# Layer two's down product in 512 columns: high and low weight parts side by side in one moving operand

## The chip, the cores and the metric

The kernel runs on one core of one Trainium2 chip. The metric is the device time of one execution in microseconds. TensorE (PE) multiplies; each product is a weight load (PEld) of the stationary operand and a MATMUL in which the moving operand streams past. VectorE (DVE) and ScalarE (ACT) do the elementwise work, GpSimd (POOL) issues the indirect DMAs, SyncE (SP) the direct ones.

## The reference, cut to what matters

Three blocks in a row over 24576 tokens (8 x 3072) of 256 features, all in float32:

```python
X = rfft(x, axis=1); y = irfft(X * (filt_r + 1j * filt_i))   # filter along the sequence
e = argmax(y @ w_gate); h = relu(y @ w1[e]); z = gate * eom * (h @ w2[e])   # layer one: 8 experts, 256 -> 1024 -> 256
h = maximum(z @ w_in, 0); out = (h * h) @ w_out   # layer two: 256 -> 2048 -> 256
```

Layer two is the one that the change touches: `w_in` is 256 x 2048 and `w_out` 2048 x 256, and both arrive as float64.

## The kernel before

Filter and routing come first, then layer one sorted by expert, then layer two over the tokens in sorted order. Layer one ends at about 1800 us of the profiled span; the rest is layer two, 48 tiles (`NTILE2`) of 512 tokens.

Every large product is made of three: an operand is split into a high part in the type that TensorE multiplies (`fp32r`) and a low part, the rest, and the kernel computes high x high + low x high + high x low. So `w_out` is held as `woh` and `wol`, and the squared activations `q` as `hh` and `hl` (line 912 on ScalarE, line 914 on VectorE).

A tile's 2048 hidden features are done in 8 units of 256 (`NU`). `steps_m` runs over the 384 units and in each step interleaves three of them, in four parts: `up2` of unit n, `split_h` of unit n-1, `down2` of unit n-2. The schedule is manual: each engine executes in the order in which the code issues, and each waits on semaphores for the data of the others.

- `up2` is a Strassen-like scheme: 7 products of 128 x 128 by 256 columns, 21 matmuls at line 881, stationary from `wsh`/`wsl`, moving from `bh`/`bl`. They go into three PSUM banks: V (`ph`), G (`px`), P (`ph`). Between them ScalarE copies (lines 888, 890, 895, 903) and VectorE adds (line 893 in part 1; lines 899 and 900 in part 2) form the four column blocks `C`. The last product of V (part 3) goes into the bank that line 899 reads, so it comes behind line 899. Line 905 (`q`, part 3) squares.
- `split_h` issues line 912 (ScalarE) in part 1 and line 914 (VectorE) in part 2, behind what `up2` issued there.
- `down2` does 24 matmuls of 256 columns at line 927. The stationary operand is a block of 128 x 128 of `hh` or `hl` (two blocks of hidden features, four blocks of tokens), the moving one a row block of `woh` or `wol`, 256 columns. The four token blocks accumulate over the tile's 8 units in two PSUM banks of 512 columns, two blocks in each; `py_tiles` alternates between two pairs of banks from tile to tile. In the last unit of a tile ScalarE copies each full bank to `ou` (line 933, 512 columns; the first is issued in part 2, the second in part 3), and GpSimd writes it out by four indirect DMAs (line 936).

The parts of `down2` end behind m = 2, 8 and 17, so parts 0 to 3 hold 3, 6, 9 and 6 of its matmuls, beside 6, 6, 6 and 3 of `up2`.

Where the operands lie: the pools on the right side of SBUF are stacked, and `open_m2` puts `pad2` (16 floats, 64 bytes) ahead of the pools of layer two. In the addresses that result, `bh`, `bl`, `hh` and `hl` of layer two begin 64 bytes past a multiple of 128, while `wsh`, `wsl`, `woh`, `wol` begin on multiples of 128. So in `up2` the moving operand is the one that is shifted, in `down2` the stationary one. In layer one (lines 802 and 819) both operands of every matmul begin on multiples of 128; there the moving operand has 512 columns in the wide tiles and 256 in the narrow ones.

Of the kernel before, what the change touches and what calls it, by code (L numbers as in the profile page):

```python
# [12 lines left out]
F32 = mybir.dt.float32  # L13
F32R = mybir.dt.float32r
# [3 lines left out]
ALU = mybir.AluOpType  # L18
# [4 lines left out]
B, S, D = 8, 3072, 256  # L23
NT = B * S
E, F1 = 8, 1024
F2 = 2048
# [4 lines left out]
TT = 512  # L31
# [71 lines left out]
def spectral_moe_kernel(ctx: ExitStack, tc: tile.TileContext, x, filt_r, filt_i, w_gate, w_og, w1, w2,  # L103
                        w_in, w_out, c_ma, c_mi, c_mb, c_mb2, c_sg, c_cum, out):
    nc = tc.nc
# [6 lines left out]
    outv = dram_disjoint_views(out, NT // 128)  # L112
# [49 lines left out]
    pl = {"xsm": ctx.enter_context(tc.tile_pool(name="xsm", bufs=2, side="right"))}  # L162
# [455 lines left out]
    w2nd, lpool = [], []  # L618
    dcs = ctx.enter_context(ExitStack())

    def decode(pool, src, parts, val=None):


        v = nc.vector
        raw = pool.tile([128, ND, 2], I32, name="raw")
        nc.sync.dma_start(out=raw, in_=src)
        yield
        H, L = raw[:, :, 1], raw[:, :, 0]
        ea = pool.tile([128, ND], I32, name="ea")
        eb = pool.tile([128, ND], I32, name="eb")  # L630
        v.tensor_scalar(ea, H, 20, 0x7FF, op0=ALU.logical_shift_right, op1=ALU.bitwise_and)
        v.tensor_scalar(eb, ea, 896, 0, op0=ALU.subtract, op1=ALU.max)
        v.tensor_scalar(ea, eb, 255, None, op0=ALU.min)
        v.tensor_scalar(eb, ea, 23, None, op0=ALU.logical_shift_left)
        yield
        v.tensor_scalar(ea, H, -2147483648, None, op0=ALU.bitwise_and)
        v.tensor_tensor(eb, ea, eb, ALU.bitwise_or)
        yield
        v.tensor_scalar(ea, H, 0xFFFFF, 3, op0=ALU.bitwise_and, op1=ALU.logical_shift_left)
        mb_ = pool.tile([128, ND], I32, name="mb_")  # L640
        v.tensor_scalar(mb_, ea, 0x3F800000, None, op0=ALU.bitwise_or)
        P = eb.bitcast(F32)
        a = pool.tile([128, ND], F32, name="a")
        v.tensor_tensor(a, mb_.bitcast(F32), P, ALU.mult)
        yield
        v.tensor_scalar(ea, L, 1, None, op0=ALU.logical_shift_right)
        lf = pool.tile([128, ND], F32, name="lf")
        v.tensor_scalar(lf, ea, 2.0 ** -51, None, op0=ALU.mult)
        v.tensor_tensor(lf, lf, P, ALU.mult)
        yield  # L650
        if val is not None:
            v.tensor_tensor(val, a, lf, ALU.add)
        for at, hi, lo in parts:
            v.tensor_tensor(hi, a[:, at], lf[:, at], ALU.add)
            v.tensor_tensor(a[:, at], a[:, at], hi.bitcast(F32), ALU.subtract)
            v.tensor_tensor(lo, a[:, at], lf[:, at], ALU.add)
        yield

    def decode_all():
        wres = ctx.enter_context(tc.tile_pool(name="wres", bufs=1))  # L660


        wsh, wsl = (wres.tile([128, F2 // 256, 7, 128], F32R, name=n) for n in ("wsh", "wsl"))
        woh, wol = (wres.tile([128, F2 // 128, D], F32R, name=n) for n in ("woh", "wol"))
        w2nd.extend((wsh, wsl, woh, wol))
        lpool.append(ctx.enter_context(tc.tile_pool(name="rp2", bufs=2)))
        pool = dcs.enter_context(tc.tile_pool(name="dcp", bufs=1))
        first, second = slice(0, 128), slice(128, 256)
        for u in range(F2 // 256):
            a0, a1 = (pool.tile([128, ND], F32, name=f"val{c}") for c in range(2))  # L670
            for c, val in enumerate((a0, a1)):
                yield from decode(pool, w_in32[c * 128:(c + 1) * 128, 2 * u * ND:2 * (u + 1) * ND]
                                  .rearrange("p (n two) -> p n two", two=2),
                                  [(at, wsh[:, u, i], wsl[:, u, i])
                                   for at, i in (((first, 0),), ((first, 1), (second, 2)))[c]], val)
            sc = pool.tile([128, 4, 128], F32, name="sc")
            v.tensor_tensor(sc[:, 0], a0[:, second], a1[:, second], ALU.add)
            v.tensor_tensor(sc[:, 1], sc[:, 0], a0[:, first], ALU.subtract)
            v.tensor_tensor(sc[:, 2], a0[:, first], a0[:, second], ALU.subtract)
            v.tensor_tensor(sc[:, 3], a1[:, first], sc[:, 1], ALU.subtract)  # L680
            yield
            nc.scalar.copy(wsh[:, u, 3:7], sc)
            v.tensor_tensor(wsl[:, u, 3:7], sc, wsh[:, u, 3:7].bitcast(F32), ALU.subtract)
            yield
        for f in range(F2 // 128):
            yield from decode(pool, w_out32[f * 128:(f + 1) * 128].rearrange("p (d two) -> p d two", two=2),
                              [(slice(0, D), woh[:, f, :], wol[:, f, :])])


    psm = ctx.enter_context(ExitStack())  # L690
# [18 lines left out]
    def py_tiles(t):  # L709
        return [pl["psY2" if t % 2 and "psY2" in pl else "psY"].tile([128, TT], F32, name=f"py{h}") for h in range(2)]  # L710
# [6 lines left out]
    slot, k = [], 0  # L717
# [120 lines left out]
    NU = F2 // 256  # L838
    R, X2, H2, Z = {}, {}, {}, {}

    def open_m2():
        right(ctx, "pad2", 1).tile([128, 16], F32, name="pad2")
        for name, bufs in (("bp", 2), ("tp2", 1), ("sp", 2), ("cp", 2), ("h2p", 3), ("oup", 2)):
            pl[name] = right(ctx, name, bufs)

    def load_t(t):
        r = lpool[0].tile([128, 2, TT], F32, name="r")
        nc.sync.dma_start(out=r, in_=ytd[:, t * TT:(t + 1) * TT].rearrange("(h p) t -> p h t", p=128))
        ix = lpool[0].tile([128, 4], I32, name="ix", bufs=4)
        nc.sync.dma_start(out=ix, in_=idsc[t * TT:(t + 1) * TT, 0:1].rearrange("(c p) o -> p (c o)", p=128))  # L850
        R[t] = r, ix
# [66 lines left out]
    def down2(t, u):  # L918

        hh, hl = H2[t, u]  # L920
        woh, wol = w2nd[2:4]
        if u == 0:
            Z[t] = [p.rearrange("p (c d) -> p c d", c=2) for p in py_tiles(t)]
        for m in range(24):
            k, i, c, n = m // 12, m // 6 % 2, m // 3 % 2, m % 3
            x, w = ((hh, woh), (hl, woh), (hh, wol))[n]
            nc.tensor.matmul(Z[t][k][:, c, :], x[:, 2 * i + k, c * 128:(c + 1) * 128], w[:, 2 * u + i, :],  # L927
                             start=u == 0 and m in (0, 12), stop=u == NU - 1 and m in (11, 23), skip_group_check=True)
            if u == NU - 1 and m in (11, 23):
                if k == 0:  # L930
                    Z[t].append(pl["oup"].tile([128, 4, D], F32, name="ou"))
                ou = Z[t][2]
                nc.scalar.copy(ou[:, 2 * k:2 * k + 2, :], Z[t][k])  # L933
                io = X2[t][2]
                for c in range(2 * k, 2 * k + 2):
                    nc.gpsimd.indirect_dma_start(out=outv[4 * t + c], out_offset=bass.IndirectOffsetOnAxis(ap=io[:, c:c + 1], axis=0),  # L936
                                                 in_=ou[:, c, :], in_offset=None)
            if m in (2, 8, 17):
                yield
        del H2[t, u]  # L940
        if u == NU - 1:
            del X2[t], Z[t]
        yield
# [59 lines left out]
    def steps_m():  # L1003
# [15 lines left out]
        m1.close()  # L1019
        xgs.close()  # L1020
        open_m2()
        st = split_t(0)
        for _ in st:
            pass
        for n in range(len(units2) + 2):
            g = up2(*units2[n]) if n < len(units2) else iter(())
            t, u = units2[min(n, len(units2) - 1)]
            d = down2(*units2[n - 2]) if n >= 2 else iter(())
            for part in range(4):
                next(g, None)  # L1030
                if part == 0 and 0 < n <= len(units2):
                    sh = split_h(*units2[n - 1])
                if part in (1, 2) and n:
                    next(sh, None)
                next(d, None)
            if u == 2 and t + 2 < NTILE2:
                load_t(t + 2)
            if u == 3 and t + 1 < NTILE2:
                st = split_t(t + 1)
            next(st, None)  # L1040
            yield
# [43 lines left out]
    m = steps_m()  # L1085
# [4 lines left out]
    for i, k in enumerate(order):  # L1090
# [3 lines left out]
        n = done["a"]  # L1094
# [24 lines left out]
    tables()  # L1119
    open_left()  # L1120
    dec.append(decode_all())
    for _ in m:
        pass
# [33 lines left out]
```

## Time and profile before

| what | value |
|---|---|
| time, median of 3 runs | 3821.22 us (3819.11 to 3822.73) |
| the profiled execution: its own time | 3831.18 us |
| its span | 3829.5 us |
| granted TensorE clock, mean | 0.994 |
| TensorE busy | 3762.7 us, 98% |
| VectorE busy | 2767.0 us, 72% |
| ScalarE busy | 1973.5 us, 52% |
| first matmul of `down2` | 1812.8 us |

The profiled execution is 10 us longer than the median of the runs, and 1.7 us longer than its own span. A busy TensorE says little by itself, since a MATMUL's length in the trace (0.28 us for 256 columns) covers its way through the array, and the next starts long before it ends. What counts for a stream of matmuls is the distance from one start to the next, which the timeline gives.

### The profile page before, as it was taken

What the parts mean: (1) busy time and instruction counts of PE and PEld (TensorE: products, weight loads), DVE (VectorE), ACT (ScalarE), POOL (GpSimd) and SP (SyncE); (2) the same over time, 40 slices, a digit from 0 to 9 for tenths busy, and PEclk for the clock granted to TensorE, in tenths of its full rate; (3) what the DMA queues carried; (4) which work ended last, traced back from release to release, by engine and by line L of the source; (5) the groups of instructions that cost most, each with busy time, mean ns of one, the idle gap of its engine ahead of it and who ended that gap; (6) DMA issues with size and microseconds to landing.
All of it is one profiled execution on the core that took longest, in us unless ns stands there. A gap on an engine that the chain in (4) does not pass through costs nothing.

```text
span 3829.5 us, 73425 instructions
## 1 busy us (share of the span) xinstructions
PE 3762.7 (98%) x27256; PEld 3512.9 (92%) x27256; DVE 2767.0 (72%) x5038; ACT 1973.5 (52%) x3909; POOL 608.2 (16%) x641
## 2 busy tenths in 40 slices
PE   8999999999999999999999999999999999999998
PEld 7888877788888888888999999999999999999998
DVE  6678685688888866655777777777777777777776
ACT  6466463354545545544555555555555555555554
POOL 3477575000000000000001100100110010011001
PEclk9999999999999999999999999999999999999999
DMA  6333322455555545543010010001001000100100
GB/s 194 100 117 113 105 86 91 142 158 165 170 163 173 178 150 161 164 148 114 23 29 23 29 29 23 29 23 29 23 29 29 23 29 23 29 23 29 29 18 18
DMA packets 262750, 309.30 MB, mean 81 GB/s; under 512 B 75153, under 2 KB 206194, under 8 KB 262386
## 3 DMA queue, kind: packets, MB, share of 16 engines
q1 hardware_dynamic: 242928, 252.39, 21.8%
q0 software_dynamic: 18432, 51.93, 3.8%
q8 instruction: 215, 3.52, 0.4%
q14 instruction: 149, 1.22, 0.1%
q10 hardware_dynamic: 1026, 0.23, 0.0%
HBM read 224.01 MB, written 80.45 MB: 80 GB/s over the span
## 4 chain that ended last, share of the span: by engine, by line
PE 37%; issue 14%; POOL 2%; DVE 0%; ACT 0%; POOLq 0%; DVEq 0%; ACTq 0%
PE py L927 20%; PE ph L881 13%; PE px L881 5%; POOL out_dram L936 2%; DVE tc L867 0%; DVE bl L871 0%; DVE hl L914 0%; DVE bl L861 0%; ACT bh L869 0%; POOLq L1152 0%; DVE C L899 0%; ACT ou L933 0%; ACT bh L860 0%; ACT u L895 0%; DVE C L900 0%
## 5 line engine op out<-in xcount | busy, mean ns | idle before, releaser
L927 PE MATMUL py<-woh,hh 128*128 128x256 f32 x3072 | 857.2, 279 | 0.0
L927 PE MATMUL py<-woh,hl 128*128 128x256 f32 x3072 | 852.8, 278 | 0.4 <-DVE hl L914 0.4
L927 PE MATMUL py<-wol,hh 128*128 128x256 f32 x3072 | 852.9, 278 | 0.0
L936 POOL DMA_INDIRECT out_dram<-ou,ix x192 | 214.0, 1115 | 2935.7 <-ACT ou L933 2891.8
L927 PEld LDWEIGHTS py<-woh,hl 128*128 128x128 f32 x3072 | 579.9, 189 | 0.9 <-DVE hl L914 0.8
L927 PEld LDWEIGHTS py<-woh,hh 128*128 128x128 f32 x3072 | 579.9, 189 | 0.0
L927 PEld LDWEIGHTS py<-wol,hh 128*128 128x128 f32 x3072 | 576.3, 188 | 0.0
L806 ACT ACTIVATE hh<-ph 128x512 fp32r<-128x512 f32 (+1 forms) x472 | 251.8, 533 | 586.3 <-PE ph L802 559.3
L881 PE MATMUL ph<-bh,wsh 128*128 128x256 f32 x1920 | 541.5, 282 | 5.6 <-ACT bh L860 4.4
L881 PE MATMUL ph<-bh,wsl 128*128 128x256 f32 x1920 | 539.2, 281 | 0.0
L881 PE MATMUL ph<-bl,wsh 128*128 128x256 f32 x1920 | 539.0, 281 | 0.0
L905 DVE SCALAR_TENSOR_TENSOR q<-C 128x1024 f32<-128x1024 f32 x384 | 468.3, 1220 | 2.3 <-ACT C L903 2.2
L808 DVE SCALAR_TENSOR_TENSOR hl<-ph,hh 128x512 fp32r<-128x512 f32 (+1 forms) x472 | 286.8, 608 | 253.4 <-ACT hh L806 248.5
L914 DVE TENSOR_TENSOR hl<-q,hh 128x1024 fp32r<-128x1024 f32 x384 | 467.1, 1217 | 1.1 <-ACT hh L912 1.1
L899 DVE TENSOR_TENSOR C<-ph,p 128x256 f32<-128x256 f32 x384 | 163.5, 426 | 417.1 <-ACT hh L912 412.8
L903 ACT COPY C<-ph 128x256 f32<-128x256 f32 x384 | 143.0, 372 | 519.7 <-PE ph L881 518.2
L912 ACT CAST hh<-q 128x1024 fp32r<-128x1024 f32 x384 | 403.1, 1050 | 1.3 <-DVE q L905 1.3
L881 PEld LDWEIGHTS ph<-bh,wsh 128*128 128x128 f32 x1920 | 363.0, 189 | 6.9 <-issue 4.6
L881 PEld LDWEIGHTS ph<-bl,wsh 128*128 128x128 f32 x1920 | 361.6, 188 | 0.0
L881 PEld LDWEIGHTS ph<-bh,wsl 128*128 128x128 f32 x1920 | 361.5, 188 | 0.0
L819 PE MATMUL py<-hh,wh 128*128 128x512 f32 (+1 forms) x944 | 348.4, 369 | 0.0
L802 PE MATMUL ph<-xh,wh 128*128 128x512 f32 (+1 forms) x944 | 340.3, 360 | 0.0
(261 smaller groups left out, 8184.2 us busy)
## 6 DMA issues: line engine op xcount, KB each, us to landing
r<-in_moe_w_dram SPq DMA_DIRECT2D x448, 256.0 KB
xt<-in_x_dram SPq DMA_DIRECT2D x48, 512.0 KB
r<-ytd SPq DMA_DIRECT2D x48, 512.0 KB
xg<-srt SPq DMA_DIRECT2D x41, 544.0 KB
ytd<-yt SPq DMA_DIRECT2D x41, 512.0 KB
xg<-srt SPq DMA_DIRECT2D x18, 272.0 KB
ytd<-yt SPq DMA_DIRECT2D x18, 256.0 KB
raw<-in_moe_w_in_dram SPq DMA_DIRECT2D x16, 256.0 KB
```

The lines of the kernel that those rows point to most:

```text
L802: nc.tensor.matmul(ps, a[:, c, f2 * 128:(f2 + 1) * 128], b[:, c, 0:w], start=n == 0, stop=n == 5)
L806: nc.scalar.activation(hh, ps, AF.Relu)
L808: nc.vector.scalar_tensor_tensor(hl, ps, 0.0, hh.bitcast(F32), op0=ALU.max, op1=ALU.subtract)
L819: nc.tensor.matmul(Y[t][h], a[:, f % 2, h * 128:(h + 1) * 128], b, start=f == 0 and i == 0, stop=f == NF - 1 and i == 2)
L881: nc.tensor.matmul(ps, x[:, u, a], y[:, b], start=start and n == 0, stop=n == 2, skip_group_check=True)
L899: nc.vector.tensor_tensor(C[:, 3], V, p5, ALU.add)
L903: nc.scalar.copy(C[:, 2], V)
L905: nc.vector.scalar_tensor_tensor(q, C, 0.0, C, op0=ALU.max, op1=ALU.mult)
L912: nc.scalar.copy(hh, q)
L914: nc.vector.tensor_tensor(hl, q, hh.bitcast(F32), ALU.subtract)
L927: nc.tensor.matmul(Z[t][k][:, c, :], x[:, 2 * i + k, c * 128:(c + 1) * 128], w[:, 2 * u + i, :], start=u == 0 and m in (0, 12), stop=u == ...
L936: nc.gpsimd.indirect_dma_start(out=outv[4 * t + c], out_offset=bass.IndirectOffsetOnAxis(ap=io[:, c:c + 1], axis=0), in_=ou[:, c, :], in_o ...
```

## The change

The two parts of `w_out` become one tile, `wo`, in which a row block's 256 high columns and 256 low columns lie side by side. `hh` now meets both in one matmul of 512 columns, whose result is 256 columns of hh x high and 256 of hh x low in one bank; `hl` meets the high half in a matmul of 256 columns that adds to the first half of the bank. So 16 matmuls replace 24, over the same number of columns (8 x 512 + 8 x 256 = 24 x 256). Each token block has a bank to itself, and every tile uses all four banks (`psY` and `psY2`). The parts now end behind m = 1, 5 and 11. In the last unit of a tile the two halves have to be added: ScalarE copies the first half to `ou` (256 columns), VectorE adds the second half to it, then GpSimd writes the block out; all this four times, the first time behind m = 5, in part 1. `open_m2` gets a second pad of 64 bytes ahead of the pools `h2p` and `oup`, which puts `hh` and `hl` on multiples of 128 bytes; `bh` and `bl` stay where they are.

```diff
--- before.py
+++ after.py
@@ -661,8 +661,8 @@
 
 
         wsh, wsl = (wres.tile([128, F2 // 256, 7, 128], F32R, name=n) for n in ("wsh", "wsl"))
-        woh, wol = (wres.tile([128, F2 // 128, D], F32R, name=n) for n in ("woh", "wol"))
-        w2nd.extend((wsh, wsl, woh, wol))
+        wo = wres.tile([128, F2 // 128, 2, D], F32R, name="wo")
+        w2nd.extend((wsh, wsl, wo))
         lpool.append(ctx.enter_context(tc.tile_pool(name="rp2", bufs=2)))
         pool = dcs.enter_context(tc.tile_pool(name="dcp", bufs=1))
         first, second = slice(0, 128), slice(128, 256)
@@ -684,7 +684,7 @@
             yield
         for f in range(F2 // 128):
             yield from decode(pool, w_out32[f * 128:(f + 1) * 128].rearrange("p (d two) -> p d two", two=2),
-                              [(slice(0, D), woh[:, f, :], wol[:, f, :])])
+                              [(slice(0, D), wo[:, f, 0], wo[:, f, 1])])
 
 
     psm = ctx.enter_context(ExitStack())
@@ -840,8 +840,10 @@
 
     def open_m2():
         right(ctx, "pad2", 1).tile([128, 16], F32, name="pad2")
-        for name, bufs in (("bp", 2), ("tp2", 1), ("sp", 2), ("cp", 2), ("h2p", 3), ("oup", 2)):
+        for name, bufs in (("bp", 2), ("tp2", 1), ("sp", 2), ("cp", 2), ("pad3", 1), ("h2p", 3), ("oup", 2)):
             pl[name] = right(ctx, name, bufs)
+            if name == "pad3":
+                pl[name].tile([128, 16], F32, name="pad3")
 
     def load_t(t):
         r = lpool[0].tile([128, 2, TT], F32, name="r")
@@ -918,24 +920,25 @@
     def down2(t, u):
 
         hh, hl = H2[t, u]
-        woh, wol = w2nd[2:4]
+        wo = w2nd[2]
         if u == 0:
-            Z[t] = [p.rearrange("p (c d) -> p c d", c=2) for p in py_tiles(t)]
-        for m in range(24):
-            k, i, c, n = m // 12, m // 6 % 2, m // 3 % 2, m % 3
-            x, w = ((hh, woh), (hl, woh), (hh, wol))[n]
-            nc.tensor.matmul(Z[t][k][:, c, :], x[:, 2 * i + k, c * 128:(c + 1) * 128], w[:, 2 * u + i, :],
-                             start=u == 0 and m in (0, 12), stop=u == NU - 1 and m in (11, 23), skip_group_check=True)
-            if u == NU - 1 and m in (11, 23):
-                if k == 0:
+            Z[t] = [pl[n].tile([128, TT], F32, name=f"py{h}") for n in ("psY", "psY2") for h in range(2)]
+        for m in range(16):
+            b, i, n = m // 8 * 2 + m // 2 % 2, m // 4 % 2, m % 2
+            w = D if n else 2 * D
+            at = 2 * i + b // 2, slice(b % 2 * 128, b % 2 * 128 + 128)
+            nc.tensor.matmul(Z[t][b][:, 0:w], (hl if n else hh)[:, at[0], at[1]],
+                             wo[:, 2 * u + i].rearrange("p s d -> p (s d)")[:, 0:w],
+                             start=u == 0 and i == 0 and n == 0, stop=u == NU - 1 and i == 1, skip_group_check=True)
+            if u == NU - 1 and i == 1 and n == 1:
+                if b == 0:
                     Z[t].append(pl["oup"].tile([128, 4, D], F32, name="ou"))
-                ou = Z[t][2]
-                nc.scalar.copy(ou[:, 2 * k:2 * k + 2, :], Z[t][k])
-                io = X2[t][2]
-                for c in range(2 * k, 2 * k + 2):
-                    nc.gpsimd.indirect_dma_start(out=outv[4 * t + c], out_offset=bass.IndirectOffsetOnAxis(ap=io[:, c:c + 1], axis=0),
-                                                 in_=ou[:, c, :], in_offset=None)
-            if m in (2, 8, 17):
+                ou = Z[t][4]
+                nc.scalar.copy(ou[:, b, :], Z[t][b][:, 0:D])
+                nc.vector.tensor_tensor(ou[:, b, :], Z[t][b][:, D:2 * D], ou[:, b, :], ALU.add)
+                nc.gpsimd.indirect_dma_start(out=outv[4 * t + b], out_offset=bass.IndirectOffsetOnAxis(ap=X2[t][2][:, b:b + 1], axis=0),
+                                             in_=ou[:, b, :], in_offset=None)
+            if m in (1, 5, 11):
                 yield
         del H2[t, u]
         if u == NU - 1:
```

## Rows read from the trace of the kernel before

**Rows 1.** The page's first part: engine, busy us (share of the span), instructions.
```profile
PE 3762.7 (98%) x27256; PEld 3512.9 (92%) x27256; DVE 2767.0 (72%) x5038; ACT 1973.5 (52%) x3909; POOL 608.2 (16%) x641
```

**Rows 2.** Busy time by stretch inside layer two; columns: stretch, length, engines.
```profile
1812.00:2740.00 928.00, 927.95 (x7973) 927.56 (x7973) 685.29 (x1063) 482.23 (x1019) 98.50 (x88) 1.00 0.09 26
2740.00:3780.00 1040.00, 1040.00 (x8944) 1039.88 (x8943) 767.41 (x1195) 541.29 (x1143) 107.24 (x96) 1.00 0.09 25
```

**Rows 3.** One of line 927's three groups: name, shape, count, busy us, mean ns, idle.
```profile
L927 PE MATMUL py<-woh,hl 128*128 128x256 f32 x3072 | 852.8, 278 | 0.4 <-DVE hl L914 0.4
```

**Rows 4.** Timeline of TensorE over one unit: start us, length us, instruction.
```profile
3021.92 0.28 PE L881 MATMUL ph<-bh,wsh 128*128 128x256 f32 x1
...
3022.62 0.28 PE L927 MATMUL py<-woh,hh 128*128 128x256 f32 x1
...
3022.96 0.28 PE L881 MATMUL ph<-bh,wsh 128*128 128x256 f32 x1
...
3023.67 0.28 PE L927 MATMUL py<-woh,hh 128*128 128x256 f32 x1
...
3024.38 0.28 PE L881 MATMUL px<-bh,wsh 128*128 128x256 f32 x1
...
3025.07 0.28 PE L927 MATMUL py<-woh,hh 128*128 128x256 f32 x1
...
3026.09 0.28 PE L881 MATMUL ph<-bh,wsh 128*128 128x256 f32 x1
...
3026.45 0.28 PE L927 MATMUL py<-woh,hh 128*128 128x256 f32 x1
...
3027.16 0.28 PE L881 MATMUL ph<-bh,wsh 128*128 128x256 f32 x1
```

**Rows 5.** Timeline of TensorE in layer one, where 256 and 512 columns meet.
```profile
1099.98 0.28 PE L802 MATMUL ph<-xh,wh 128*128 128x256 f32 x1
...
1101.42 0.40 PE L802 MATMUL ph<-xh,wh 128*128 128x512 f32 x1
...
1102.82 0.28 PE L819 MATMUL py<-hh,wh 128*128 128x256 f32 x1
...
1103.53 0.39 PE L802 MATMUL ph<-xh,wh 128*128 128x512 f32 x1
```

**Rows 6.** Timeline of TensorE in layer one, 512 columns alone.
```profile
1107.02 0.39 PE L819 MATMUL py<-hh,wh 128*128 128x512 f32 x1
...
1111.10 0.39 PE L802 MATMUL ph<-xh,wh 128*128 128x512 f32 x1
```

**Rows 7.** Timeline of ScalarE in the unit of rows 4, which ends a tile.
```profile
3023.92 0.37 ACT L895 COPY u<-ph 128x256 f32<-128x256 f32 x1 [0.68 <-PE ph L881]
3024.19 1.05 ACT L912 CAST hh<-q 128x1024 fp32r<-128x1024 f32 x1
3025.61 0.59 ACT L933 COPY ou<-py 128x512 f32<-128x512 f32 x1 [0.37 <-PE py L927]
3026.70 0.37 ACT L903 COPY C<-ph 128x256 f32<-128x256 f32 x1 [0.51 <-PE ph L881]
```

**Rows 8.** Timeline of VectorE in the same unit.
```profile
3025.34 0.43 DVE L899 TENSOR_TENSOR C<-ph,p 128x256 f32<-128x256 f32 x1 [1.33 <-ACT hh L912]
3025.68 0.41 DVE L900 TENSOR_TENSOR C<-px,u 128x256 f32<-128x256 f32 x1
3026.01 1.22 DVE L914 TENSOR_TENSOR hl<-q,hh 128x1024 fp32r<-128x1024 f32 x1
3027.15 1.22 DVE L905 SCALAR_TENSOR_TENSOR q<-C 128x1024 f32<-128x1024 f32 x1
```

**Rows 9.** Timeline of the kernel's end.
```profile
3818.43 0.96 POOL L936 DMA_INDIRECT out_dram<-ou,ix  x1 [32.80 <-ACT ou L933]
...
3818.67 0.28 PE L927 MATMUL py<-wol,hh 128*128 128x256 f32 x1
...
3822.22 0.96 POOL L936 DMA_INDIRECT out_dram<-ou,ix  x1 [0.30 <-issue]
```

## The prediction, made before the changed kernel was run

> **What bounds the kernel now.** First the page's busy shares [rows 1]: TensorE 98%, VectorE 72%, and nothing else above 52% but the weight loads. Second, the busy time by stretch [rows 2]: in layer two TensorE is busy 927.95 of 928.00 and 1040.00 of 1040.00 us at a granted clock of 1.00, while VectorE is busy for about 74% and the DMAs move 26 GB/s. So there TensorE issues without a gap, and whatever shortens or holds up its stream of matmuls is paid in full. Third, the groups [rows 3]: line 927 has three groups of 3072 matmuls, so 24 in each of 384 units, with 0.4 us of idle time ahead of them. Fourth, as busy lengths overlap, the distance between starts [rows 4]: one unit runs from 3021.92 to 3027.16, 5.24 us for 45 matmuls, 116.4 ns each. 384 such units are 2012 us, over half of the kernel.
>
> Within the unit the distance isn't constant. The reader is to take the differences: up2's four groups take 0.70, 0.71, 0.69 and 0.36 us for 6, 6, 6 and 3 matmuls (2.46 us), down2's take 0.34, 0.71, 1.02 and 0.71 for 3, 6, 9 and 6 (2.78 us). 1.02/9 is 113.3 ns, 0.71/6 is 118.3: the same instruction comes at a tight spacing or at a loose one. Up2's third group follows a loose group of down2 and is tight (115), its second and fourth follow tight ones and are loose (118, 120).
>
> **The rate of the new matmuls.** Columns stay at 6144 per unit and all operands keep their type; only the count falls from 24 to 16. Layer one shows what 512 columns cost with both operands on multiples of 128 bytes, as after the change: alone, 18 in 4.08 us [rows 6], 226.7 ns, which is twice 113.3. So 512 columns cost just what two tight matmuls of 256 do; nothing is saved by the instruction as such, only the loose spacing can be. Layer one also shows the price of the alignment: 12 matmuls of 256 columns there take 1.44 us [rows 5], 120.0 each, worse than either spacing of layer two, where one operand is shifted. And where the two widths meet, six of 512 take 1.40 us (233.3 each) and the six of 256 behind them 0.71 (118.3).
>
> The new down2 alternates the widths one by one, which no row shows. Bounds: all tight, 8 x (226.7 + 113.3) = 2.72 us, 0.06 under today's 2.78, over 384 units a gain of 23 us; at the worst of the rows, 8 x (233.3 + 120.0) = 2.83 us, a loss of 18 us. The nearest row is where the widths meet: 8 x (233.3 + 118.3) = 2.81 us, 0.03 more than now: +12 us. I take this one.
>
> The Trainium skill, "TensorE: Matmul & The Clock Gate", section "Back-to-back issue gap", gives a matmul its columns at 2.4 GHz and 2.5 ns besides; by that alone 8 fewer would give back 20 ns per unit, an estimated 8 us. The rows for 512 and 256 columns show no fixed part (226.7 against 2 x 113.3), so here the trace disagrees. The skill's "SBUF — State Buffer", section "Who interferes with whom", has TensorE wait on nobody for SBUF; read so, 64 bytes of shift couldn't matter. The 120.0 ns against 113.3 for the same shape speak against that reading.
>
> **What it does to up2.** Its matmuls and addresses stay. By the pattern above a group of up2 behind a loose group of down2 is tight. If the new down2 is loose throughout, as just taken, up2's second and fourth groups become as tight as the first and third: four groups of 0.70, 0.69, 0.69 and 0.35 (half of 0.69) against 0.70, 0.71, 0.69 and 0.36, 0.03 us per unit or -10 us. Bounds: all 21 at 113.3 (2.38, -31 us) and all at 118.3 (2.48, +8 us).
>
> **The step at a tile's end.** This part is certain in kind. Before, ScalarE copied two banks of 512 columns, 0.59 us each [rows 7], and VectorE had no part in it. Now ScalarE makes four copies of 256 columns, at 0.37 like line 895 [rows 7], and VectorE four additions from PSUM, at 0.42 like lines 899 and 900 [rows 8]. ScalarE is idle enough: 0.3 us more in a tile of 42. VectorE gets 1.7 us more per tile, which its idle quarter (1.3 us per unit) swallows within two units. But the order counts. The first copy and addition are issued behind m = 5, in part 1, ahead of part 2's lines 899 and 900 on VectorE, and behind line 912 on ScalarE, a long one. From rows 7 and 8:
> - line 912 runs from 3024.19 to 3025.24; the bank is ready earlier (m = 5 stands where the sixth matmul of the group from 3023.67 stands, which ends by about 3024.6). So the copy goes from about 3025.2 to 3025.55.
> - The first addition starts 0.08 behind it (as line 905 starts at 3027.15 behind line 903's end at 3027.07), at 3025.65.
> - Line 899, which now starts at 3025.34, follows 0.34 behind that (the distance of 899 and 900), at 3026.0 instead of 3025.34: about 0.65 late, done at 3026.4.
> - Up2's last product starts at 3026.09 [rows 4] and must wait for line 899, which now ends at 3025.77, 0.3 ahead. With 0.08 for the semaphore and one weight load (a matmul's distance, 0.11) behind 3026.4 it starts at 3026.6. TensorE stands for 0.5 us; bounds 0.4 to 0.6, by ScalarE's overlap of two instructions (0.10 between lines 895 and 912).
>
> The last tile has no up2 beside it, so 47 x 0.5 = 23.5 us (19 to 28). Behind the stalled matmul wait only the last four matmuls of down2 and the next unit, all on the path. What else is late: line 914 by 0.65 us, but its result is first read in the next unit's part 0, one slot later than now since the 512-column matmul stands before it; line 905 by some 1 us with the second addition ahead of it, but line 912 of the next unit, which waits for it, is then 0.5 us later itself by the stall, and starts on time. The other three additions have no reader but the DMAs and the bank. The four banks are now used by every tile: bank 0 is read out 4 us before its next use, the last one, by additions behind line 905, some 1 us ahead of its own (m = 10 of the next unit). I cost that at nothing; if the cover is gone, it's up to 0.4 us more per tile, one addition, 19 us. Lower bound for the whole step: 0, if line 899 isn't held.
>
> **The rest.** The decoding writes the same columns to other places: nothing. The DMAs keep count and size, and GpSimd is idle before them (32.80 us in rows 9). At the end four indirect DMAs follow one another from 3818.43 to 3823.18 [rows 9]; the first block is ready a little earlier, the last not late: -0.3 to 0, taken as 0.
>
> **Sum** against the profiled execution: 3831.2 + 12 - 10 + 23.5 = 3857 us. That execution lies 10 us above the median of the runs, so for the median: 3821.2 + 25.5 = 3847 us. On the rates I have one analogue and the sign of a pattern; they nearly cancel, and the step at the tile's end is what decides.
>
> **Rivals.**
> - Tight: in the new stream 512-column matmuls leave the weight loads time to spare, the spacing settles as in rows 6, and both products run at 113.3 per 256 columns: -23 - 31 = -54 us, with the stall of 23.5 left: 3791 us, faster. For it: the 18 regular distances in rows 6, reached behind a disturbed stretch of the same kind. Against it: a matmul of 256 columns between each two, which in rows 5 goes to 118 to 120. It decides from the point where both products together save 0.061 us per unit (23.5/384) of the 0.14 that there is (0.06 and 0.08).
> - Halfway: tight 512s, 256s as loose as where the widths meet, up2 as taken: 8 x (226.7 + 118.3) = 2.76, -8 - 10 + 23.5 = +6 us, 3827 us, no change that can be told.
> - The stall isn't there: ScalarE's copy gets done before line 899 is due, or the addition doesn't hold VectorE. Against it stands the plain order of issue. With the rates taken: 3823 us.
> - Loose everywhere: pairs at 2.83 and up2 all at 118.3, and the banks come late: 18 + 8 + 23.5 + 10 = +60 us, 3881 us. For it: rows 5's 120.0, the only row of 256 columns at this alignment.
>
> **How the numbers follow.** Chances: forecast 0.50, tight 0.24, halfway or no stall 0.17, loose everywhere 0.09. 0.2% of this time, 8 us, is about what a measurement tells from no change. The forecast's own range is 3832 to 3862 (stall 19 to 28, rates -10 to +13), all slower. From the tight case I take in down to 3793, from loose everywhere up to 3868: this leaves about 2 in 10 out. Faster: the tight case and a part of the cases without a stall, 0.29; within 0.2%: 0.16; slower: 0.55.
>
> **What would show it.** In the profile after: a group of L899's idle time released by line 912 or the new copy, and some 47 waits of TensorE for VectorE's line 899, 0.5 us each; a busy share of TensorE a little under 1.00 in layer two; starts of 512 columns 227 or 233 ns apart, of 256 columns 113 or 118 to 120; 0.35 us for up2's last product if it is tight. The prediction is wrong if line 899's successor on TensorE doesn't wait at a tile's end, or if a unit inside a tile (free of the stall) is shorter than 5.17 us.

## The result, and the profile after

The changed kernel takes 3843.55 us (median of 5 runs, 3842.24 to 3845.28) against 3821.22: a ratio of 1.0058, 95% interval 1.0046 to 1.007. The forecast was 3847, range 3793 to 3868, slower.

The two profiled spans, 3829.5 and 3842.1 us, are only 12.6 us apart, because the execution profiled before lay 10 us above its median, and that excess stands ahead of layer two: down2's first matmul came at 1812.8 us there and at 1800.3 in after. So the stage itself has to be compared.

From `open_m2` on, lines of the kernel after stand two or three further down: up2's matmuls are line 883 there (881 before), V's addition, line 899, is 901, the casts to `hh` and `hl`, lines 912 and 914, are 914 and 916, and down2's matmuls are line 930. The new copy is line 937, the new addition 938.

Line 930's rows of after (least, median and greatest length in ns, then first and last start) give the stage's length:

```profile
L930 PE MATMUL py<-wo,hh x3072: 387/392/400, 1800.3 to 3831.2; 128*128 128x512 f32 x192
L930 PE MATMUL py<-wo,hl x3072: 276/281/388, 1800.6 to 3831.4; 128*128 128x256 f32 x192
```

From the first to the last matmul of down2 these are 2031.1 us. Before they were 1812.8 to 3818.67 [rows 9], 2005.9. The stage is 25.2 us longer. The medians are only 22.3 apart; down2's first matmul began anywhere from 1796 to 1814 us in the profiled executions of this case, so a few us either way ahead of the stage say nothing of the change. Where the 25.2 are, two views show. First, busy time by stretch, of after and then of the first experiment below, which has the same matmuls without the stall:

```profile
2740.00:3780.00 1040.00, 1038.18 (x7258) 964.08 (x7257) 790.20 (x1277) 541.34 (x1178) 118.66 (x96) 1.00 0.08 25
```

```profile
2740.00:3780.00 1040.00, 1040.00 (x7317) 972.11 (x7316) 796.65 (x1285) 545.41 (x1187) 119.68 (x98) 1.00 0.09 25
```

Before, 8944 matmuls in 1040 us [rows 2], 45 to a unit, make 5.233 us per unit. In the first experiment's kernel 7317, 37 to a unit, make 5.259. So the undisturbed unit is 0.026 us longer: 10 us over 384. The 59 matmuls by which after falls short of that in this stretch are the stall. Second, the chain of waits of after over the end of one tile (start, length, what), where the forecast had put it:

```profile
2813.47 0.71 PE ph L883 x6
...
2814.26 0.09 ACT u L897
...
2814.53 1.05 ACT hh L914
2815.58 0.28 ACT ou L937
...
2815.88 0.42 DVE ou L938
2816.31 0.34 DVE C L901
2816.65 0.04 issue
2816.69 0.62 PE ph L883 x3
2817.32 0.69 PE py L930 x4
```

The reader is to follow it down: up2's product, ScalarE's long line 914, then the new copy, the new addition, line 901 behind the addition, and only then up2's last product. Elsewhere in this stretch the chain stays on TensorE. The same from the timeline, ScalarE, VectorE, the weight load and TensorE:

```profile
2815.48 0.86 ACT L937 COPY ou<-py 128x256 f32<-128x256 f32 x2
2816.23 0.41 DVE L901 TENSOR_TENSOR C<-ph,p 128x256 f32<-128x256 f32 x1
2816.69 0.19 PEld L883 LDWEIGHTS ph<-bh,wsh 128*128 128x128 f32 x1 [0.39 <-DVE C L901]
2816.35 0.28 PE L930 MATMUL py<-wo,hl 128*128 128x256 f32 x1
2816.69 0.39 PE L883 MATMUL ph<-bh,wsh 128*128 128x256 f32 x1
2816.92 0.28 PE L883 MATMUL ph<-bl,wsh 128*128 128x256 f32 x1
```

The waits of the whole stage (who waited for whom, us in total, times, longest) show how often this happens:

```profile
DVE ou L938 <- ACT ou L937: 72.1, 47, 1.8
PEld ph L883 <- DVE C L901: 19.1, 50, 0.7
```

Of the 50, 47 stand at the ends of tiles, 42.4 us apart and 0.39 us each with few exceptions; the other three are inside tiles, 0.2 us each.

The distances inside a tile, from one unit of after:

```profile
3013.91 0.29 PE L883 MATMUL ph<-bh,wsh 128*128 128x256 f32 x1
...
3014.61 0.39 PE L930 MATMUL py<-wo,hh 128*128 128x512 f32 x1
...
3014.96 0.28 PE L883 MATMUL ph<-bh,wsh 128*128 128x256 f32 x1
...
3015.65 0.39 PE L930 MATMUL py<-wo,hh 128*128 128x512 f32 x1
...
3016.35 0.28 PE L883 MATMUL px<-bh,wsh 128*128 128x256 f32 x1
...
3017.06 0.39 PE L930 MATMUL py<-wo,hh 128*128 128x512 f32 x1
...
3018.12 0.29 PE L883 MATMUL ph<-bh,wsh 128*128 128x256 f32 x1
...
3018.48 0.39 PE L930 MATMUL py<-wo,hh 128*128 128x512 f32 x1
...
3019.17 0.29 PE L883 MATMUL ph<-bh,wsh 128*128 128x256 f32 x1
```

The answer to rows 4: up2's groups take 0.70, 0.69, 0.71 and 0.36 (2.46 us, as before), down2's 0.35, 0.70, 1.06 and 0.69 (2.80, before 2.78).

### The profile page after: what moved, and what is told of

The parts are those of the page before. It is cut to its first block, busy times and chain, and to the rows that moved or that the text cites. A ratio compares the mean times of both kernels' runs of the same rounds, so it can differ in the third digit from the quotient of the medians.

```text
span 3842.1 us, 67659 instructions
## 1 busy us (share of the span) xinstructions
PE 3780.5 (98%) x24184; PEld 3387.3 (88%) x24184; DVE 2829.8 (74%) x5230; ACT 1989.5 (52%) x4005; POOL 634.1 (17%) x641
## 4 chain that ended last, share of the span: by engine, by line
PE 49%; ACT 2%; issue 1%; DVE 1%; POOL 0%; ACTq 0%; POOLq 0%; DVEq 0%
PE py L930 25%; PE ph L883 17%; PE px L883 6%; ACT hh L914 1%; DVE ou L938 1%; DVE C L901 0%; ACT ou L937 0%; ACT u L897 0%; POOL out_dram L939 0%; ACTq L937 0%; DVE tc L869 0%; POOLq L1155 0%; DVE bl L873 0%; DVE bl L863 0%; ACT bh L871 0%
## 5 line engine op out<-in xcount | busy, mean ns | idle before, releaser
L930 PE MATMUL py<-wo,hh 128*128 128x512 f32 x3072 | 1140.2, 392 | 0.0
L930 PE MATMUL py<-wo,hl 128*128 128x256 f32 x3072 | 864.6, 281 | 0.4 <-DVE hl L916 0.4
L939 POOL DMA_INDIRECT out_dram<-ou,ix x192 | 240.0, 1250 | 2934.0 <-DVE ou L938 2903.5
L930 PEld LDWEIGHTS py<-wo,hh 128*128 128x128 f32 x3072 | 578.3, 188 | 64.1
L930 PEld LDWEIGHTS py<-wo,hl 128*128 128x128 f32 x3072 | 576.6, 188 | 1.0 <-DVE hl L916 1.0
L883 PE MATMUL ph<-bh,wsh 128*128 128x256 f32 x1920 | 549.5, 286 | 8.7 <-ACT bh L862 4.2
L802 PE MATMUL ph<-xl,wh 128*128 128x512 f32 (+1 forms) x944 | 338.1, 358 | 0.7 <-DVE xl L787 0.7
L819 PE MATMUL py<-hl,wh 128*128 128x512 f32 (+1 forms) x944 | 338.2, 358 | 0.0
```

What stands on the lines that cost most here:

```text
L802: nc.tensor.matmul(ps, a[:, c, f2 * 128:(f2 + 1) * 128], b[:, c, 0:w], start=n == 0, stop=n == 5)
L819: nc.tensor.matmul(Y[t][h], a[:, f % 2, h * 128:(h + 1) * 128], b, start=f == 0 and i == 0, stop=f == NF - 1 and i == 2)
L883: nc.tensor.matmul(ps, x[:, u, a], y[:, b], start=start and n == 0, stop=n == 2, skip_group_check=True)
L930: nc.tensor.matmul(Z[t][b][:, 0:w], (hl if n else hh)[:, at[0], at[1]], wo[:, 2 * u + i].rearrange("p s d -> p (s d)")[:, 0:w], start=u == ...
L939: nc.gpsimd.indirect_dma_start(out=outv[4 * t + b], out_offset=bass.IndirectOffsetOnAxis(ap=X2[t][2][:, b:b + 1], axis=0), in_=ou[:, b, :] ...
```

## Experiments

Medians of the kernel before were 3819 to 3832 us in the sets of runs, so each time is told beside the one of before in its own set, with the ratio and its interval. "Unit" is 1040 us divided by the matmuls from 2740 to 3780 us, times those in a unit.

### 1. The order of issue at a tile's end

```diff
-            if u == NU - 1 and i == 1 and n == 1:
-                if b == 0:
+            if u == NU - 1 and m in (7, 13, 15):
+                if m == 7:
...
+                for b in {7: (0, 1), 13: (2,), 15: (3,)}[m]:
```

> The changed kernel with the copies and additions of a tile's first two blocks issued behind m = 7 (part 2, behind VectorE's lines 901, 902 and 916) instead of behind m = 5 and m = 7; the same instructions otherwise. Theory (the order of issue is what holds TensorE at a tile's end): the 0.32 us by which a tile's last unit is longer go, 47 x 0.32 = 15 us, so about 3828 us, and units inside a tile stay at 5.26 us. Rival (VectorE's extra load or the banks hold it, whatever the order): a tile's last unit stays at 5.58 and the time within 4 us of 3843.

3826.32 us beside 3818.93: 1.0018 (1.0009 to 1.0027). TensorE is busy for all of the stretch (the second row by stretch above), and its waits for line 901 are gone but one:

```profile
PEld ph L883 <- DVE C L901: 0.2, 1, 0.2
```

Layer two is 2015.4 us long, 15.7 shorter than in the changed kernel. VectorE does the same additions, and the four banks are used in the same way. So it was the order of issue, and the rival falls. The new copies and additions as such cost nothing that can be told: a tile's last unit is then as long as the others, 5.26 us.

### 2. The pad, the order of widths, the alignment alone

The changed kernel without `pad3`:

```diff
-        for name, bufs in (... ("cp", 2), ("pad3", 1), ("h2p", 3), ("oup", 2)):
+        for name, bufs in (... ("cp", 2), ("h2p", 3), ("oup", 2)):
```

> The changed kernel without the second pad: hh and hl lie 64 bytes past a multiple of 128 again, 16 matmuls as in the change. Theory (the spacing of starts is set by where both operands lie and by what the matmul before was): down2's pairs of 512 and 256 move, by rows of before towards 226.7 + 115.9 = 342.6 ns against 349.8 now, 8 x 384 x 7 ns = 22 us less, about 3821; up2 moves too. Rival (the pad is of no effect, TensorE's reads don't meet): within 4 us of 3843. The stall at a tile's end stays in both.

3841.32 beside 3818.93: 1.0058 (1.0045 to 1.0072). The rival's answer: in this form, with the first pad in place, the second does nothing that can be told.

The changed kernel with the widths in groups:

```diff
-            b, i, n = m // 8 * 2 + m // 2 % 2, m // 4 % 2, m % 2
+            b, i, n = ((0, 0, 0), (0, 0, 1),
+                       (1, 0, 0), (0, 1, 0), (1, 0, 1), (0, 1, 1),
+                       ...
```

> The changed kernel with each part's 512-column matmuls first and its 256-column ones behind them, the parts and their counts as they are. Theory (a 512 behind a 512 goes to 226.7, a 256 between two of them disturbs it): down2 falls from 2.80 us per unit towards 8 x (226.7 + 118.3) = 2.76, 15 us less, about 3828. Rival (a disturbed start costs the same in any order): within 4 us of 3843. The stall at a tile's end stays in both.

3840.63 beside 3818.93: 1.0056 (1.0042 to 1.0069). The rival again: groups of two or three are no better than turns.

The kernel before with `pad3` alone:

```diff
-        for name, bufs in (... ("cp", 2), ("h2p", 3), ("oup", 2)):
+        for name, bufs in (... ("cp", 2), ("pad3", 1), ("h2p", 3), ("oup", 2)):
```

> The kernel before with the second pad alone: 24 matmuls of 256 columns, both operands on multiples of 128. Theory (alignment sets the spacing, 120.0 ns as in layer one): down2 goes from 2.78 to 2.88 us per unit, +38 us, about 3859. Rival (no effect of the alignment): within 4 us of 3821.

3838.73 beside 3818.93: 1.005 (1.0037 to 1.0064), a unit of 5.286 us (8854 matmuls). Both miss: alignment costs 20 us where down2 has 256 columns, half of what layer one's 120.0 would make. Down2 takes 2.84 us per unit there, 118.3 ns a matmul and not 120.0, although both its operands lie on multiples of 128.

### 3. Where the two operands lie, in both products at once

The moving operands 64 bytes off, the stationary ones on multiples of 128, in the kernel before (and with `pad3`), and the same in the first experiment's kernel:

```diff
+        wres.tile([128, 16], F32, name="pad4")
         woh, wol = (wres.tile([128, F2 // 128, D], F32R, name=n) for n in ("woh", "wol"))
```

> The kernel before with the second pad and 64 bytes of pad ahead of woh: in both products of layer two the moving operand lies 64 bytes past a multiple of 128 and the stationary one on a multiple, so that also where up2 and down2 follow one another a matmul's moving operand and the next one's weights lie 64 bytes apart. Theory (the loose spacing comes in where the two lie alike, which is at the changes between up2 and down2): the units settle at the tight spacing, 45 x 113.4 = 5.10 us against 5.23, 51 us less, about 3768; or, where the loose spacing holds itself, at 45 x 117.5 = 5.29, about 3840, one of the two and nothing between. Rival (the changes of tiles and banks as such disturb, wherever operands lie): 5.22 to 5.30 with up2's groups beginning 122, 116, 114 as now.

> The first experiment's kernel (changed form, first copy behind m = 7) with 64 bytes of pad ahead of wo, so that in both products the moving operand lies 64 bytes past a multiple of 128 and the stationary one on a multiple. Theory (alike addresses bring the loose spacing): 512s at 226.7, 256s at 113.4, unit 5.10 us against 5.26, about 3765 to 3770 us. Rival (the change of width disturbs by itself): 512s at 224 to 237 in turn, unit 5.2 to 5.3, within 10 us of 3826.

All operands on multiples of 128, in the kernel before:

```diff
-        right(ctx, "pad2", 1).tile([128, 16], F32, name="pad2")
```

> The kernel before without the first pad: all operands of layer two on multiples of 128, as in layer one. Theory (alike addresses set 120.0 ns, as layer one's narrow tiles show): 45 x 120 = 5.40 us per unit against 5.23, +64 us, about 3883. Rival (only changes between differently placed streams disturb, so a uniform placement is tight): 5.10 us, about 3770.

The rows by stretch, first of the kernel before with unlike places, then of the one with like places:

```profile
2740.00:3780.00 1040.00, 1040.00 (x8820) 1039.92 (x8819) 758.90 (x1180) 536.90 (x1128) 107.02 (x96) 1.00 0.09 25
```

```profile
2740.00:3780.00 1040.00, 1040.00 (x8669) 1039.93 (x8667) 750.33 (x1157) 527.22 (x1107) 106.81 (x96) 1.00 0.08 25
```

Like places: 1040/8669 is 119.97 ns, the 120.0 of layer one at every place in the unit, and 3882.75 us beside 3820.89: 1.016 (1.0146 to 1.0174), as the theory had it (3883). Unlike places: 117.9 ns, a unit of 5.306, 3845.97 us: 1.0069 (1.0055 to 1.0082). By its mean that is nearest the theory's second case, but it isn't one spacing that holds itself: the single distances run from 114 to 123 ns, and no group runs at 113. The rival's reason fails too, as up2's groups no longer begin with 122, 116, 114 (part 0's begins with 117, 119, 117). In the changed form unlike places give 3819.62 us beside 3820.89: 0.9996 (0.9987 to 1.0005), a unit of 5.240 (7344 matmuls). The theory's 5.10 was missed by far, and the rival's range was right. That the change of width is what disturbs isn't shown by it, since with this placement a stream of one width isn't tight either.

### 4. Other distances

The same pads cut to place the moving operand 32 or 96 bytes past a multiple of 128 (for 32: `pad2` 24 floats, `pad3` and `pad4` 8; for 96: 8, 24 and 24).

> The kernel before with other pads: in both products of layer two the moving operand lies 32 bytes past a multiple of 128, the stationary one on a multiple. At 0 bytes the unit took 5.40 us, at 64 bytes 5.31. Theory (how far apart the two lie within 128 bytes sets the spacing, and a stream keeps the spacing in which it is): one spacing throughout, a value of its own between 113.4 (5.10 us, about 3769) and 120 ns (5.40, 3883). Rival (only like or unlike halves of 128 bytes count): as with like halves, 5.40, since 32 bytes leave both in the same half.

> The same with the moving operand 96 bytes past a multiple of 128. Theory (distance within 128 bytes): a value of its own between 5.10 and 5.40 us per unit, not that of 32 bytes, if the order of the two matters. Rival (halves of 128 bytes): as at 64 bytes, 5.31 us, about 3846.

> The first experiment's kernel (changed form, first copy behind m = 7) with the moving operand of both products 32 bytes past a multiple of 128 and the stationary one on a multiple. At 64 bytes this form took 5.24 us per unit and 3820 us, with the change's own placement 5.26 and 3826. Theory: it follows the 24-matmul form at 32 bytes: where that is tighter than 5.31 us, this is below 5.24 and so below both kernels. Rival (the change of width sets the spacing): 5.23 to 5.27, 3818 to 3828 us.

At 32 bytes the kernel before takes 3857.11 beside 3830.53, 1.0069 (1.0052 to 1.0086), with 8820 matmuls in the stretch, as many as at 64; at 96 bytes 3864.28, 1.0087 (1.007 to 1.0104), a unit of 5.326 (8787). Neither a value for each distance (32 and 64 bytes have the same) nor one for each half (32 isn't like 0): 0 bytes stands alone with 120.0, the three others are close to 118. The changed form at 32 bytes takes 3850.72, 1.0054 (1.0037 to 1.0071), a unit of 5.294 (7268). The theory's condition isn't met, as 5.306 is no tighter than 5.31, and the rival's 5.23 to 5.27 is missed.

### 5. The swap, and a try for more

If uniform places never give 113, what gave it before? Both kernels below have the placement of before and only other parts.

```diff
-            if m in (2, 8, 17):
+            if m in (8, 11, 20):
```

> The kernel before with down2's 24 matmuls split over the parts as 9, 3, 9 and 3 instead of 3, 6, 9 and 6; placement and all else as before. Theory (with the placement of before, each change from down2 to up2 swaps the spacing between tight and loose, so that parts 0 and 2 are tight and 1 and 3 loose): 30 of 45 matmuls are tight instead of 24, 6 x 4.2 ns = 0.025 us per unit, 5.21 us against 5.23, 10 us less than before; with the swap the other way round, 5.26 us, 10 us more. Rival (the spacing is tied to operands or banks, not to what went before): within 3 us of before and the single matmuls keep their spacing.

```diff
-            if m in (2, 8, 17):
+            if m in (2, 8, 20):
```

> The kernel before with down2's matmuls split as 3, 6, 12 and 3: three move from part 3, which is loose there, to part 2, which is tight; no wait gets shorter cover than it had. Theory (the spacing swaps at each change from down2 to up2 and otherwise stays): part 2's down2 keeps 113 for all 12, part 3's first three keep 118, 3 x 4.2 ns = 0.013 us per unit, 5.22 us and 5 us less than before; with the swap the other way round about 5.26 us and 10 us more. Rival (spacing tied to the operands): the three keep 118 and the time stays within 2 us.

Parts of 9, 3, 9, 3: 3880.06 beside 3831.57, 1.0123 (1.0106 to 1.0139), a unit of 5.366 (8722 matmuls). One unit:

```profile
2642.34 0.28 PE L881 MATMUL ph<-bh,wsh 128*128 128x256 f32 x1
...
2643.05 0.28 PE L927 MATMUL py<-woh,hh 128*128 128x256 f32 x1
...
2644.11 0.28 PE L881 MATMUL ph<-bh,wsh 128*128 128x256 f32 x1
...
2644.80 0.28 PE L927 MATMUL py<-woh,hh 128*128 128x256 f32 x1
...
2645.14 0.28 PE L881 MATMUL px<-bh,wsh 128*128 128x256 f32 x1
...
2645.95 0.28 PE L927 MATMUL py<-woh,hh 128*128 128x256 f32 x1
...
2647.01 0.29 PE L881 MATMUL ph<-bh,wsh 128*128 128x256 f32 x1
...
2647.36 0.28 PE L927 MATMUL py<-woh,hh 128*128 128x256 f32 x1
...
2647.70 0.28 PE L881 MATMUL ph<-bh,wsh 128*128 128x256 f32 x1
```

Down2's groups take 1.06, 0.34, 1.06 and 0.34 us for 9, 3, 9 and 3: 118, 113, 118 and 113 ns each, where before it was 113, 118, 113 and 118 [rows 4]. So the spacing did swap at every change from down2 to up2, the other way round. Only 15 of 45 matmuls are tight, 9 fewer than before; at 4.2 ns each that is 0.04 us, a unit of 5.27 (the expectation's 5.26 for this case counted six). The rest is a wait that the expectation overlooked: with three matmuls of down2 in part 1, only six stand between V's second and third product, too few for line 895's copy. ScalarE's row, then TensorE's:

```profile
2645.06 0.37 ACT L895 COPY u<-ph 128x256 f32<-128x256 f32 x1 [1.38 <-PE ph L881]
```

```profile
2645.38 0.28 PE L881 MATMUL px<-bh,wsl 128*128 128x256 f32 x1
2645.50 0.37 PE L881 MATMUL ph<-bh,wsh 128*128 128x256 f32 x1
2645.71 0.28 PE L881 MATMUL ph<-bl,wsh 128*128 128x256 f32 x1
```

The copy ends at 2645.43, the weight load of 2645.50's product begins at 2645.48, and the matmul behind it comes after 0.21 instead of 0.12: 0.09 us in each unit, 35 us. The waits don't list this one, as the load's engine was hardly idle; that the copy holds it is read from these times.

Parts of 3, 6, 12, 3: 3838.79 beside 3819.78, 1.0054 (1.004 to 1.0068). Five or six of a tile's eight units are 5.22 us long, with 113 throughout part 2, just as the theory says; two are 5.45 to 5.50, where ScalarE's line 888, on which V's next product waits, stands behind casts for a coming tile (line 869's, 1.06 us from 2622.06, and line 860's three, 1.02 us from 2653.64), for which the shorter part 3 leaves less time:

```profile
PEld ph L881 <- ACT s L888: 16.5, 92, 0.2
```

That no wait had shorter cover was my error; the 5 us of gain were there and some 24 us of stalls beside them. No version tried here beats the kernel before beyond its interval.

## Why the prediction was right

The direction, the place and the sum hold: 25.5 us forecast, 25.2 measured in the stage and 22.3 between the medians. The terms agree less well than the sum.

- **Bound.** Right: layer two is TensorE's stream, and what held or loosened it there showed in the time.
- **The step at a tile's end.** Right in kind, shown by experiment 1; mis-sized: 47 x 0.5 = 23.5 us forecast, 15.7 measured (47 x 0.33, under the lower bound of 19). The forecast's times, 3026.4 + 0.19 - 3026.09, make 0.50. Told from the unit's start (3021.92 in rows 4, 2812.26 in after), line 901 ends at 4.38 us and not at 4.48: the copy starts 0.10 ahead of line 914's end, where I had only 0.04, and the addition 0.03 behind the copy, where my times had 0.10. The stalled matmul starts 0.05 behind line 901, not 0.19, but the next one comes 0.23 behind it instead of 0.12: 0.16 in place of 0.19. And the stalled matmul was due 0.04 later, as the matmuls ahead of it in the unit run a little later than in rows 4. 0.50 - 0.10 - 0.03 - 0.04 = 0.33.
- **The rate of down2.** +12 us forecast, about 6 measured (medians over all units from their starts: 2.798 us in the first experiment's kernel, 2.781 before). That 512 columns bring no gain as such held; the widths taking turns cost about what rows 5 show. The reason that I had added, that like places are the dearer ones, was not the cause here: without the pad (experiment 2) the time is the same. The 2.5 ns that the prediction takes from the Trainium skill, "TensorE: Matmul & The Clock Gate", section "Back-to-back issue gap", are given there for a matmul by itself and not for a stream with weight loads, so the 8 us worked out from them don't apply here.
- **up2.** Wrong: -10 us forecast, +4 measured (2.462 us against 2.452, in the same way). That a group of up2 is tight behind a loose group of down2, and loose behind a tight one, holds in the kernel before, where experiment 5 shows it with other parts too. It doesn't hold behind alternating widths: in the unit of after the first two groups come at 0.70 and 0.69 and the last two at 0.71 and 0.36, still two of four.
- **The cover.** Right: no wait of TensorE for the additions or copies of a bank shows in after, and the other three additions cost nothing that can be told.
- **Rivals.** The tight case had its chance only by the analogue of rows 6; not even opposed places brought it about (experiment 3). Without the stall the time is 7 us above before (experiment 1); the rival had 2, with up2's gain in it.

So two overestimates, of the stall (8 us) and of down2's loss (6 us), made up for the gain of up2 that didn't come (14 us). That the sum comes out to 0.3 us is luck. Two sums of the prediction are a little off, without bearing on this: 0.03 us per unit of up2 are 11.5 us, not 10, and the forecast's own range begins at 3830, not 3832.

What stays open: why the spacing swaps at the change from down2 to up2 and not at the change back (in the placement of before a matmul's moving operand and the next one's weights lie alike at both), why it doesn't behind alternating widths, and why the other placements stay near 118. The runs show that it is so, not the mechanism.

## What to carry to other kernels

When a step is added behind work of the same engine, look for the instruction that now queues behind it and who waits for that one: here an addition of 0.42 us, issued one part too early, cost 0.33 us of the busiest engine per tile, and issuing it later gave that back for nothing. Before making matmuls wider, compare the distance between starts at both widths: if it is proportional, there is nothing in the width itself. Before shortening one part of an interleaved schedule, recount what covers each wait on the other engines.

## What the runs showed of the hardware that wasn't expected

With one granted clock (1.00) and TensorE busy throughout, groups of matmuls of 256 columns came at a mean distance of 113.3, about 118 or 120.0 ns. 120.0 came for all 45 matmuls of a unit when the operands of both products began on multiples of 128 bytes, and for a whole unit with no other placement tried; with down2's operands alone there, down2 came at 118.3. A matmul whose weight load had to wait starts almost at once behind the load's begin, but is longer (0.37 to 0.39 us instead of 0.28), and the next start comes 0.21 to 0.23 us later instead of 0.12: part of the price of a wait stands behind the waiting matmul, where the waits don't show it.
